# Chunk-selected attention and a soft mixture of experts: combining weights by one exponential, slot maxima in two bf16 parts, slot outputs by column halves

## The chip, the cores and the metric

The kernel is one program on one core of a Trainium2 chip. The metric is the device time of one execution in microseconds (us), as the median of several runs; a measurement of this kernel can tell a difference of about 0.2% from no change. All durations of single instructions come from one profiled execution, which has a time of its own. The engines are PE (matrix multiplication; PEld is its weight loading), DVE (VectorE), ACT (ScalarE), POOL (GpSimd) and SP (SyncE, which here only issues transfers).

## The reference: what is computed

Attention over 4 batches of 8 heads, 768 positions of width 64; each query sees only the keys of its 6 best chunks of 32 (by an upper bound of the score), and causally. The result `x` (3072 rows of 512) goes through a soft mixture of 8 experts with 4 slots each:

```python
logits = x @ phi                                  # 3072 x 32 slots
d = np.exp(logits - logits.max(0))                # dispatch: softmax over rows, for each slot
d /= d.sum(0) + 1e-09
slot_input = (d.T @ x).reshape(E, S_per_e, D)     # 8 experts x 4 slots x 512
for e in range(E):
    h = np.maximum(slot_input[e] @ w1[e], 0.0)    # 512 -> 1024
    slot_out[e] = h @ w2[e]                       # 1024 -> 512
c = np.exp(logits - logits.max(1))                # combine: softmax over slots, for each row
c /= c.sum(1) + 1e-09
return c @ slot_out                               # 3072 x 512, fp32
```

## The kernel before

**The body.** Sixteen pairs of heads, four for each batch, run through one software pipeline. For each pair: transposes of k and q, chunk bounds, selection (MAX8 on DVE), scores on PE, exponentials on ACT, causal masks on POOL, the product with v on PE, normalisation on DVE. The order of the steps is written out by hand as strings (L712 to L717): `PLAIN`, `LOGITS`, `SLOTS`, `AFTER` in turn, `BEFORE_LAST` and `FINAL` for the last two pairs. Each engine works its own instructions in just that order, so an instruction that waits holds all behind it on its engine.

**The mixture's steps in the body.** When a batch's four pairs are through, its mixture steps are sown into the strings. `moe_logits` forms the logits, `moe_copy` (L451, L452) their maximum for each partition, `pm_pad`, and a copy. In the next pair `moe_max` (L458) transposes `pm_pad` on PE in fp32, `moe_bound` (L465) reduces it to `mb`, one value for each slot, and `moe_exp` (L471) spreads `mb` over all partitions by an fp32 matmul with the identity and takes the running maximum (L476, L478). `moe_comb` (L506, L508) subtracts each row's maximum, `moe_comb2` calls `exp_c`, which writes the combining weights; `moe_dispatch` (L531, L535) forms the slot inputs. This is done for batches 0, 1 and 2 at about 53, 81 and 110 us. The last batch goes through its own code behind the last pair (L804 to L839), where `mneg` (L811) is the negated maximum, spread by fp32 matmuls into the logits themselves (L820) and into `bc` (L825).

**The combining weights' layout.** The 32 slots of a row don't stand next to each other in what is multiplied later. `c_pad` has four groups of 32 columns for each row tile. In group j, columns 0 to 3 hold expert j, 4 to 11 experts 4 + j and 5 + j, 12 to 15 expert 4. The same slot thus stands in several places: a slot's output may be summed up from parts that four column groups of PE form side by side, and where no part is formed the factor is zero. `live` marks the lanes of which each slot's sum of weights is taken once.

**The tail.** `experts_in` (L873) multiplies the slot inputs by w1, `relu` (L880) and `hidden_T` (L885, L889) give the transposed hidden values in `hT_pad`. Three functions then form the slot outputs, 512 columns in two halves `y` of 256: `experts_out` (L912) for experts 0 to 3, both halves in one matmul of 512 columns into `so_ps`; `shared_out` (L937) for experts 5 to 7, whose work is shared out over the four column groups; `last_expert_out` (L947) for expert 4. Half 1 goes on into `so_ps`, half 0 into `so_last`. `hidden_T` has two parts `f`, and so have the first two functions. `slot_sums` (L893) gives `zinv`, the inverse of the dispatch sums, from `zrow`, which DVE (L854) and POOL (L859, L860) fill in the layout above. When half 1 is complete, ACT scales it (L992) and stores what `experts_out` left of half 0 (L993, `so_part`); `out_half` then multiplies it by the combining weights of six double tiles of rows (L981), scales them on DVE and ACT (L970, L967) and writes each from SP (L983). Then follows half 0 for the same rows, closed by DVE's fused multiply-add (L1000), and then the other rows with all 512 columns (L1010, L1014, L1016).

The order of that stretch, which the change rewrites:

```python
    experts_out(0)
    hidden_T(1)
    shared_out(1, 0)
    slot_sums()
    experts_out(1)
    shared_out(1, 1)
    last_expert_out(1)
```

Of the kernel before, what the change touches and what calls it, by code (L numbers as in the profile page):

```python
# [59 lines left out]
def kernel(  # L60
# [21 lines left out]
    LAST = NPAIR - 1  # L82

# [36 lines left out]
    pm_pad = static.tile([P, P], F32, name="pm_pad")  # L120
    ns_t = [static.tile([P, NJ, 2, 2, CH], BF16, name=f"ns_t{i}") for i in range(2)]
# [325 lines left out]

    def moe_copy(b):
        lg = small.tile([P, NQT, NS], F32, name="lg", tag="lg")
        ps = st.pop(("lgps", b))  # L450
        nc.vector.tensor_reduce(pm_pad[:, :NS], ps.rearrange("p t s -> p s t"), axis=AX.X, op=ALU.max)  # L451
        nc.vector.tensor_copy(lg, ps)  # L452
        st["lg", b] = lg

    def moe_max(b):

        pmT = p_tp.tile([P, P], F32, name="pmT_ps", tag="tp")
        nc.tensor.matmul(pmT, lhsT=pm_pad, rhs=identf, is_transpose=True)  # L458
        st["pmT", b] = pmT

    def moe_bound(b):
# [4 lines left out]
        st["mb", b] = mb  # L466

    def moe_exp(b):
        lg = st.pop(("lg", b))
        bc = p_tp.tile([P, NS], F32, name="bc_ps", tag="tp")  # L470
        nc.tensor.matmul(  # L471
            bc, lhsT=st.pop(("mb", b)).broadcast_to([P, P]), rhs=identf[:, :NS], start=True, stop=True,
        )
# [40 lines left out]
    def exp_c(lc):  # L514
        c4 = lc[:, :NQT].rearrange("p t (j s) -> p t j s", s=SPE)
        nc.scalar.activation(c_pad[:, :, :, :SPE], c4[:, :, :4], func=ACT.Exp)
# [112 lines left out]
    load_w(1)  # L629

# [18 lines left out]
    nc.vector.memset(pm_pad, 0.0)  # L649
    qneg(2)  # L650
    qpos(2)

    def step(i, what):
# [47 lines left out]
        else:  # L701
# [3 lines left out]
                "moe_max": moe_max, "moe_bound": moe_bound, "moe_comb": moe_comb, "moe_exp": moe_exp,  # L705
# [7 lines left out]
    LOGITS = """sc:0 trk sc:2 ex:0 ex:2 ub norm sc:3 evk lv mk:0 ex:3 pv:0 pv:5 mk:2 pv:1 sc:1 sel xt trq pv:2:3 ex:1 evq sc:5 ex:5 mk:1 kmin sc:4 evx ns moe_logits@2 lw kmax bd evns mk:3 qsn ex:4 mk:5 mk:4 pv:4 lkq moe_copy@2 qsp"""  # L713
    SLOTS = """sc:0 ex:0 moe_max@3 mk:0 sc:1 ex:1 mk:1 ub moe_bound@3 norm sel trk moe_comb@3 evk sc:2 pv:0 pv:1:2 lkq ex:2 sc:3 moe_exp@3 ex:3 mk:3 trq xt pv:3 kmin mk:2 evqd moe_exp2@3 evx kmax bd moe_scale@3 lw sc:4 ex:4 lv mk:4 sc:5 moe_comb2@3 ex:5 mk:5 ns pv:5:4 evns moe_dispatch@3 qsn qsp"""
# [4 lines left out]
    for i in range(1, NPAIR):  # L719
        if i >= EARLY:  # L720
# [94 lines left out]
    def cinv(n):  # L815
# [3 lines left out]
    rep = identf[:NS, :NS].rearrange("p (o s) -> p o s", o=1)  # L819
    nc.tensor.matmul(  # L820
        lg2, lhsT=mneg.broadcast_to([NS, P]), rhs=rep.broadcast_to([NS, NQT, NS]),
        start=False, stop=True, skip_group_check=True,
    )
# [28 lines left out]
    for g in range(2):  # L852
        sl = slice(g * 16, (g + 1) * 16)
        nc.vector.tensor_tensor(  # L854
            zrow[:, :, g * SPE:(g + 1) * SPE],
            si_acc[:1, NDG, sl].rearrange("p (j s) -> p j s", j=4),
            z[:1, sl].rearrange("p (j s) -> p j s", j=4), op=ALU.add,
        )
# [23 lines left out]
    def hidden_T(f):  # L882
# [3 lines left out]
        for g in range(2):  # L886
            o = hT_pad[:, f * 4:(f + 1) * 4, g * 4:(g + 1) * 4, g * SPE:(g + 1) * SPE]
# [15 lines left out]
    so_ps = p_at.tile([P, 2, 512], F32, name="so_ps", tag="at")[:, 0, :]  # L903
    so_last = p_sc.tile([P, HD], F32, name="so_last", tag="sc")
    so_part = tail.tile([P, HD], F32, name="so_part")
# [3 lines left out]
    def experts_out(f):  # L909
        for fg in range(f * 4, (f + 1) * 4):  # L910
            for e in range(4):
                nc.tensor.matmul(  # L912
                    so_ps[e * CH:(e + 1) * CH, :], lhsT=hT_pad[:, fg, e, :],
                    rhs=w_sb[E + e][:, fg * Dm:(fg + 1) * Dm], start=(fg == 0), stop=(fg == NFG - 1),
                )

    outs = (so_last, so_ps[:, HD:])
# [7 lines left out]

    def shared_out(y, f):
        for n in range(3):
            for j in range(4):
                e, fg = SHARED[j][n]
                fg += f * 4  # L930
                c0 = e * CH - (SPE if j == e - 5 else 0)
                if e == LATE[-2]:
                    rhs = w_half[e, y][:, fg, :]
                else:
# [5 lines left out]
                    start=(y == 0 and f == 0 and n == 0), stop=False, skip_group_check=(y == 1),  # L940
                )

    def last_expert_out(y):
        c0 = 4 * CH - 2 * SPE
        for fg in range(NFG):
            j = fg % 4
            nc.tensor.matmul(  # L947
                outs[y][j * CH:(j + 1) * CH, :], lhsT=hT[:, fg, c0:c0 + CH],
                rhs=w_half[LATE[-1], y][:, fg, :],
                start=False, stop=(fg >= NFG - 4), skip_group_check=(y == 1),  # L950
# [34 lines left out]
    experts_out(0)  # L985
    hidden_T(1)
    shared_out(1, 0)
    slot_sums()
    experts_out(1)
# [59 lines left out]
```

## Time and profile before

| | |
|---|---|
| median of 3 runs | 158.46 us (158.31 to 158.50) |
| profiled execution, whole | 158.78 us |
| its span | 157.1 us |
| PE, DVE, ACT, POOL busy | 87%, 77%, 77%, 62% of the span |
| combining exponentials of a batch (L516, L519, L520) | 0.27, 0.35, 0.27 us on ACT |
| PE's transpose of the maxima (L458), three times | 0.33 us each |
| PE's spreading of the maxima (L471), three times two passes | 0.29 us for a pass |
| row writes from SP | 14 of 256 KB, 5 of 512 KB |

A row of the timeline gives the start, the duration, the engine, the line, the operation and what it writes and reads; in brackets stands the engine's idle time ahead of it and what ended it. PE's ends are modelled and matmuls overlap, so the starts of successive ones tell more than the durations. A row of the chain of waits gives start, duration, engine, tile and line. A row of the stretches gives, for each engine, its busy time and its number of instructions, then PE's granted clock, the share of the DMA engines, and GB/s.

### The profile page before, as it was taken

To read this page: it belongs to the slowest core of one execution; us is meant where nothing else is said; L and a number is where in the kernel's file an instruction comes from. 1 tells how busy PE (TensorE), PEld (TensorE's weight loads), DVE (VectorE), ACT (ScalarE), POOL (GpSimd) and SP (SyncE) were. 2 spreads that over 40 slices of the span, in tenths; PEclk is the share of its full clock that TensorE was granted. 3 is DMA by queue.
4 is the path that set the end of the run, shared out by engine and by line. 5 is a ranking of instruction groups with operands and counts; after the bars stand their busy time and mean duration, and the time that the engine had idled before them with its cause. 6 is when DMAs were issued, how large, how long until landed. Compare 5 with 4: busy or idle time off the path is not lost.

```text
span 157.1 us, 6041 instructions
## 1 busy us (share of the span) xinstructions
PE 137.4 (87%) x2485; PEld 91.1 (58%) x2486; DVE 121.6 (77%) x442; ACT 121.2 (77%) x172; POOL 97.8 (62%) x196
## 2 busy tenths in 40 slices
PE   7866799999999999999999999999998999877700
PEld 5543456767666676756657676767666854444200
DVE  4758789889899899999989999989952761178820
ACT  3557899999999988999979789998879531277600
POOL 7899861975878786493868866678598780000000
PEclk9999999999999999999999999999999999999975
DMA  5999999999999999999999999999999999949995
GB/s 152 188 187 211 178 210 213 164 192 215 197 209 196 209 194 211 204 220 172 195 173 211 206 214 177 215 195 214 208 206 212 208 194 197 131 169 384 400 422 230
DMA packets 46171, 33.31 MB, mean 212 GB/s; under 512 B 26304, under 2 KB 41664, under 8 KB 46144
## 3 DMA queue, kind: packets, MB, share of 16 engines
q0 software_dynamic: 41328, 25.86, 113.5%
q1 hardware_dynamic: 4816, 7.08, 12.2%
q8 instruction: 19, 0.31, 0.7%
q14 instruction: 8, 0.07, 0.1%
HBM read 52.49 MB, written 6.29 MB: 374 GB/s over the span
## 4 chain that ended last, share of the span: by engine, by line
PE 58%; DVE 22%; ACT 7%; issue 3%; POOL 3%; DMA 2%; DVEq 0%; POOLq 0%; ACTq 0%
PE at_ps L398 11%; PE sc_ps L346 11%; PE sc_ps L356 8%; PE tr_ps L238 6%; ACT e_sb L370 4%; PE xT_ps L420 3%; PE ub_ps L296 3%; DVE mx L317 3%; DVE x_sb L411 3%; ACT o_sb L967 3%; PE h_ps L873 2%; DVE mm L256 2%; DVE mm L262 2%; DMA w_sb<-in_k_dram 2%; PE ns_ps L328 2%
## 5 line engine op out<-in xcount | busy, mean ns | idle before, releaser
L370 ACT ACTIVATE e_sb<-sc_ps 128x768 bf16<-128x768 f32 (+1 forms) x96 | 83.1, 926 | 6.5 <-PE sc_ps L356 5.1
L380 POOL TENSOR_SCALAR_AFFINE_SELECT e_sb<-e_sb 128x256 bf16<-128x256 bf16 x96 | 37.9, 417 | 22.0 <-ACT e_sb L370 21.8
L346 PE MATMUL sc_ps<-qT,kT 64*128 64x384 bf16 (+3 forms) x258 | 37.5, 308 | 2.3 <-ACT e_sb L370 2.0
L356 PE MATMUL sc_ps<-nsT,smask 64*128 64x384 bf16 (+2 forms) x294 | 37.7, 284 | 0.3
L398 PE MATMUL at_ps<-v_t,e_sb 128*128 128x65 bf16 x642 | 27.1, 194 | 0.4 <-DVE x_sb L411 0.2
L398 PEld LDWEIGHTS <-e_sb 128*128 128x128 bf16 x642 | 22.8, 97 | 6.5 <-POOL e_sb L380 2.9
L317 DVE MAX8 mx<-ub_ps 128x8 f32<-128x8 f32 (+1 forms) x192 | 16.9, 164 | 5.8 <-PE ub_ps L306 4.9
L346 PEld LDWEIGHTS <-kT 64*128 64x128 bf16 x258 | 12.6, 93 | 9.5 <-issue 3.5
L356 PEld LDWEIGHTS <-smask 64*128 64x128 bf16 x294 | 14.7, 95 | 3.8 <-issue 1.3
L169 POOL DMA_DIRECT2D v_t<-in_v_dram x16 | 16.6, 1041 | 0.2
L411 DVE TENSOR_TENSOR x_sb<-at_ps,inv 128x768 bf16<-128x768 f32 (+1 forms) x17 | 15.5, 910 | 0.6
L247 ACT COPY kT<-tr_ps 128x768 bf16<-128x768 bf16 x16 | 12.8, 802 | 3.5 <-PE tr_ps L238 3.5
L256 DVE TENSOR_REDUCE mm<-kT 128x24 bf16<-128x768 bf16 x16 | 15.1, 944 | 0.4 <-ACT kT L247 0.4
L262 DVE TENSOR_REDUCE mm<-kT 128x24 bf16<-128x768 bf16 x16 | 15.1, 943 | 0.0
L247 ACT COPY qT<-tr_ps 128x768 bf16<-128x768 bf16 x14 | 11.5, 823 | 3.3 <-PE tr_ps L238 3.3
L145 POOL DMA_DIRECT2D w_sb<-in_moe_w_dram x14 | 10.2, 729 | 0.0
L296 PEld LDWEIGHTS <-qpn 128*128 128x128 bf16 x192 | 6.0, 96 | 6.7 <-issue 3.3
L431 DVE COPY xT_sb<-xT_ps 128x768 bf16<-128x768 bf16 (+1 forms) x15 | 8.0, 536 | 2.2 <-PE xT_ps L420 2.0
L296 PE MATMUL ub_ps<-bd,qpn 128*128 128x48 bf16 x192 | 7.8, 184 | 1.6 <-POOL qpn L276 1.4
L238 PE MATMUL tr_ps<-ident,k_in 128*64 128x128 bf16 x192 | 8.4, 223 | 0.7 <-DVE k_in L585 0.5
L420 PE MATMUL xT_ps<-ident,x_sb 128*128 128x128 bf16 x96 | 8.2, 220 | 0.3 <-DVE x_sb L411 0.3
L238 PE MATMUL tr_ps<-ident,q_in 128*64 128x128 bf16 x192 | 8.4, 223 | 0.0
(155 smaller groups left out, 216.3 us busy)
## 6 DMA issues: line engine op xcount, KB each, us to landing
w_sb<-in_moe_w_dram POOLq DMA_DIRECT2D x14, 1024.0 KB, 12.7
out_dram<-o_sb SPq DMA_DIRECT2D x14, 256.0 KB, 2.5
v_t<-in_v_dram POOLq DMA_DIRECT2D x16, 192.0 KB, 10.6
k_in<-in_k_dram POOLq DMA_DIRECT2D x7, 384.0 KB, 9.3
q_in<-in_q_dram POOLq DMA_DIRECT2D x7, 384.0 KB, 10.4
out_dram<-o_sb SPq DMA_DIRECT2D x5, 512.0 KB, 4.0
w_half<-in_moe_w_dram POOLq DMA_DIRECT2D x8, 256.0 KB, 11.5
w_sb<-in_k_dram SPq DMA_DIRECT2D x1, 384.0 KB, 3.3
```

The source lines that it names most:

```text
L238: nc.tensor.matmul(ps[h * 64:(h + 1) * 64, g, :], lhsT=src[:, h, g * D:(g + 1) * D], rhs=ident, is_transpose=True,)
L247: copy(t.rearrange("d (p g) -> d p g", g=NQT), st.pop((nm + "ps", i)).rearrange("d g p -> d p g"),)
L256: nc.vector.tensor_reduce(mm[:, 0, 0, :], kT, axis=AX.X, op=ALU.min)
L262: nc.vector.tensor_reduce(mm[:, 1, 0, :], kT, axis=AX.X, op=ALU.max)
L296: nc.tensor.matmul(o, lhsT=qpn[:, x, t * P:(t + 1) * P], rhs=bd[:, x], start=(t == 0 and x == 0), stop=False,)
L317: nc.vector.max(mx[:, a, :], ub[:, a, :max(8, 4 * t + 4)])
L346: nc.tensor.matmul(ps[:, h, c:c + w], lhsT=kT[r, kg * P:(kg + 1) * P], rhs=qT[r, qs], start=True, stop=False,)
L356: nc.tensor.matmul(ps[:, h, c + (f - t0) * P:c + (l - t0) * P], lhsT=smask[r, x, kg].rearrange("p a b -> p (a b)"), rhs=nsT[r, (f - x * NJ ...
L370: nc.scalar.activation(e[:, :, :w], st.pop(("scps", i, g))[:, :, :w], func=ACT.Exp, scale=scale)
L380: nc.gpsimd.affine_select(out=e[:, :, c:c + P], in_=e[:, :, c:c + P], compare_op=ALU.is_ge, fill=0.0, base=0, pattern=[[0, 2], [1, P]], ch ...
L398: nc.tensor.matmul(o, lhsT=st["e", i, g][:, h, c:c + P], rhs=v_t[i % NV][:, h, kg, :D + 1], start=(kg == 0), stop=(kg == t),)
L411: nc.vector.tensor_tensor(st["x", b][:, t0:t1, 2 * j:2 * j + 2, :].rearrange("p t h d -> p h t d"), at[:, :, :, :D], inv.broadcast_to([P, ...
```

## The change

Three edits, with what they need.

*One exponential for the combining weights.* `exp_c` writes 24 neighbouring columns for group j: the logits of experts j to j + 5, by one overlapping read. The place of expert e in group j is therefore always 4 (e - j); `window` gives the matching place in `hT_pad`, in which experts 4 to 7 now stand 16 columns in. `live` marks columns 0 to 3 and 16 to 19 of each group; it is built on POOL from `once` and reduced on DVE ahead of the sixth pair. `zrow` is filled by two DVE additions with overlapping reads, without POOL.

*Maxima in two bf16 parts.* The upper 16 bits of an fp32 value are a bf16 (`high`); the rest, `pm_lo`, `mb_lo` or `mneg_lo`, is one more DVE subtraction. The transposes and the spreading matmuls become two bf16 matmuls that add up.

*Halves apart.* `experts_out` takes the half as an argument and forms 256 columns. Everything of half 1 is formed first; half 0 follows after half 1's six output tiles, all of it. `so_part` goes, and half 0 is closed by a plain scaling.

```diff
+    WIN, HOME = 6 * SPE, 4 * SPE
...
-    nc.vector.memset(live, 0.0)
     nc.vector.memset(lc_sb[:, NQT], 0.0)
-    for j in range(4):
-        nc.vector.memset(live[j * CH:j * CH + 2 * SPE, :], 1.0)
...
+    def high(t):
+        return t.bitcast(BF16).rearrange("p (s x) -> p s x", x=2)[:, :, 1]
...
+    def moe_lo(b, eng=nc.vector):
+        eng.tensor_tensor(pm_lo[:, :NS], pm_pad[:, :NS], high(pm_pad)[:, :NS], op=ALU.subtract)
...
-        nc.tensor.matmul(pmT, lhsT=pm_pad, rhs=identf, is_transpose=True)
+        nc.tensor.matmul(pmT, lhsT=high(pm_pad), rhs=ident, start=True, stop=False)
+        nc.tensor.matmul(pmT, lhsT=pm_lo, rhs=ident, start=False, stop=True)
...
-        st["mb", b] = mb
+        mb_lo = small.tile([P, 1], BF16, name="mb_lo", tag="mb_lo")
+        nc.vector.tensor_tensor(mb_lo, mb, high(mb), op=ALU.subtract)
+        st["mb", b] = high(mb), mb_lo
...
-        nc.tensor.matmul(
-            bc, lhsT=st.pop(("mb", b)).broadcast_to([P, P]), rhs=identf[:, :NS], start=True, stop=True,
-        )
+        for n, part in enumerate(st.pop(("mb", b))):
+            nc.tensor.matmul(
+                bc, lhsT=part.broadcast_to([P, P]), rhs=ident[:, :NS], start=(n == 0), stop=(n == 1))
...
-        c4 = lc[:, :NQT].rearrange("p t (j s) -> p t j s", s=SPE)
-        nc.scalar.activation(c_pad[:, :, :, :SPE], c4[:, :, :4], func=ACT.Exp)
-        pairs = c4[:, :, 4:8]
-        pairs = bass.AP(pairs.tensor, pairs.offset, [list(x) for x in pairs.ap[:-1]] + [[1, 2 * SPE]])
-        nc.scalar.activation(c_pad[:, :, :, SPE:3 * SPE], pairs, func=ACT.Exp)
-        nc.scalar.activation(
-            c_pad[:, :, :, 3 * SPE:4 * SPE], c4[:, :, 4:5].broadcast_to([P, NQT, 4, SPE]), func=ACT.Exp)
+        c4 = lc[:, :NQT].rearrange("p t (j s) -> p t j s", s=SPE)[:, :, :4]
+        runs = bass.AP(c4.tensor, c4.offset, [list(x) for x in c4.ap[:-1]] + [[1, WIN]])
+        nc.scalar.activation(c_pad[:, :, :, :WIN], runs, func=ACT.Exp)
...
+    once = static.tile([P, 8], BF16, name="once")
+    nc.gpsimd.memset(once, 1.0)
+    for sign, base in ((1, 0), (-1, SPE - 1)):
+        nc.gpsimd.affine_select(
+            out=once, in_=once, compare_op=ALU.is_ge, fill=0.0, base=base,
+            pattern=[[-sign * HOME, 8]], channel_multiplier=sign,
+        )
...
     nc.vector.memset(pm_pad, 0.0)
+    nc.vector.memset(pm_lo, 0.0)
...
-    LOGITS = """... lkq moe_copy@2 qsp"""
-    SLOTS = """sc:0 ex:0 moe_max@3 mk:0 sc:1 ..."""
+    LOGITS = """... lkq moe_copy@2 moe_lo@2 qsp"""
+    SLOTS = """sc:0 ex:0 mk:0 moe_max@3 sc:1 ..."""
...
+        if i == NPB + 1:
+            nc.vector.tensor_reduce(live, once, axis=AX.X, op=ALU.max)
...
-    nc.tensor.matmul(
-        lg2, lhsT=mneg.broadcast_to([NS, P]), rhs=rep.broadcast_to([NS, NQT, NS]),
-        start=False, stop=True, skip_group_check=True,
-    )
+    mneg_lo = small.tile([NS, 1], BF16, name="mneg_lo", tag="mneg_lo")
+    nc.vector.tensor_tensor(mneg_lo, mneg, high(mneg), op=ALU.subtract)
     bc = p_tp.tile([P, NS], F32, name="bc_ps", tag="tp")
-    nc.tensor.matmul(
-        bc, lhsT=mneg.broadcast_to([NS, P]), rhs=identf[:NS, :NS], start=True, stop=True,
-    )
+    for n, part in enumerate((high(mneg), mneg_lo)):
+        nc.tensor.matmul(
+            lg2, lhsT=part.broadcast_to([NS, P]), rhs=rep.broadcast_to([NS, NQT, NS]),
+            start=False, stop=(n == 1), skip_group_check=True,
+        )
+        nc.tensor.matmul(
+            bc, lhsT=part.broadcast_to([NS, P]), rhs=ident[:NS, :NS], start=(n == 0), stop=(n == 1),
+        )
...
-    nc.gpsimd.tensor_copy(zrow[:, :3, 2 * SPE:3 * SPE], zrow[:, 1:, SPE:2 * SPE])
-    nc.gpsimd.tensor_copy(
-        zrow[:, :, 3 * SPE:4 * SPE], zrow[:, :1, SPE:2 * SPE].broadcast_to([1, 4, SPE]))
+    for n, c, w in ((4, 0, WIN - SPE), (3, WIN - SPE, SPE)):
+        nc.vector.tensor_tensor(
+            zrow[:, :n, c:c + w], windows(si_acc[:1, NDG, :], n, c, w), windows(z[:1], n, c, w), op=ALU.add)
...
-    so_ps = p_at.tile([P, 2, 512], F32, name="so_ps", tag="at")[:, 0, :]
+    so_ps = p_at.tile([P, 2, 512], F32, name="so_ps", tag="at")[:, 0, :HD]
...
-    def experts_out(f):
+    outs = (so_last, so_ps)
+
+    def experts_out(y, f):
         for fg in range(f * 4, (f + 1) * 4):
             for e in range(4):
+                w0 = fg * Dm + y * HD
                 nc.tensor.matmul(
-                    so_ps[e * CH:(e + 1) * CH, :], lhsT=hT_pad[:, fg, e, :],
-                    rhs=w_sb[E + e][:, fg * Dm:(fg + 1) * Dm], start=(fg == 0), stop=(fg == NFG - 1),
+                    outs[y][e * CH:(e + 1) * CH, :], lhsT=hT_pad[:, fg, e, :],
+                    rhs=w_sb[E + e][:, w0:w0 + HD], start=(fg == 0), stop=False,
                 )
...
+    def window(e, j):
+        return e * CH + HOME - (e - j) * SPE
...
-    experts_out(0)
+    experts_out(1, 0)
+    shared_out(1, 0)
     hidden_T(1)
-    shared_out(1, 0)
     slot_sums()
-    experts_out(1)
+    experts_out(1, 1)
     shared_out(1, 1)
     last_expert_out(1)
-    nc.scalar.activation(so_sb[1], so_ps[:, HD:], func=ACT.Copy, scale=zinv)
-    nc.scalar.activation(so_part, so_ps[:, :HD], func=ACT.Copy, scale=zinv)
+    nc.scalar.activation(so_sb[1], outs[1], func=ACT.Copy, scale=zinv)
     TAGS = (("tp", "tp"), ("sc", "at"))
     for m in range(BYHALF):
         out_half(m, 1, TAGS[m % 2])
-    shared_out(0, 0)
-    shared_out(0, 1)
+    for f in range(2):
+        experts_out(0, f)
+    for f in range(2):
+        shared_out(0, f)
     last_expert_out(0)
-    nc.vector.scalar_tensor_tensor(so_sb[0], so_last, zinv, so_part, op0=ALU.mult, op1=ALU.add)
+    nc.vector.tensor_scalar_mul(so_sb[0], outs[0], zinv)
```

More of the change, by code (lines that the diff above doesn't have):

```diff
@@ L851, with windows @@
     nc.vector.tensor_reduce(z[:1], st.pop("zt")[:1].rearrange("p t s -> p s t"), axis=AX.X, op=ALU.add)
[L852 to L853 removed]
+    def windows(t, n, c, w):
+        return bass.AP(t.tensor, t.offset + c, [list(t.ap[0]), [SPE, n], [1, w]])
+    for n, c, w in ((4, 0, WIN - SPE), (3, WIN - SPE, SPE)):
         nc.vector.tensor_tensor(
[L855 to L858, printed above, removed]
[L859 to L861 removed]
+            zrow[:, :n, c:c + w], windows(si_acc[:1, NDG, :], n, c, w), windows(z[:1], n, c, w), op=ALU.add)
     cT = cT_all.rearrange("p (m a) (c x) -> p m x (a c)", a=2, x=2)
@@ L930, in shared_out @@
                 fg += f * 4
-                c0 = e * CH - (SPE if j == e - 5 else 0)
+                c0 = window(e, j)
                 if e == LATE[-2]:
@@ L939, in shared_out @@
                     rhs=rhs,
-                    start=(y == 0 and f == 0 and n == 0), stop=False, skip_group_check=(y == 1),
+                    start=False, stop=False,
                 )
     def last_expert_out(y):
-        c0 = 4 * CH - 2 * SPE
         for fg in range(NFG):
             j = fg % 4
+            c0 = window(LATE[-1], j)
             nc.tensor.matmul(
```

15 lines of the change are left out of this document (7 added, 8 removed).

## The prediction

> **What bounds the kernel now.** I read the chain of waits first, then, from the end backwards, the stretches of the output phase, SyncE's queue and the timeline of the tail, and last the three places where the softmax maxima are formed.
>
> ```profile
> span 157.1 us, 6041 instructions
> PE 58%; DVE 22%; ACT 7%; issue 3%; POOL 3%; DMA 2%; DVEq 0%; POOLq 0%; ACTq 0%
> 139.50:139.75 0.25, 0.25 (x3) 0.01 (x1) 0.25 (x1) 0.15 (x2) 0.00 (x0) 1.00 0.37 135
> 139.75:140.00 0.25, 0.25 (x13) 0.24 (x16) 0.25 (x2) 0.25 (x2) 0.00 (x0) 1.00 1.08 385
> 145.00:146.00 1.00, 0.10 (x4) 0.10 (x5) 0.84 (x2) 0.10 (x1) 0.00 (x0) 1.00 1.09 381
> 155.25:155.50 0.25, 0.00 (x0) 0.00 (x0) 0.00 (x0) 0.00 (x0) 0.00 (x0) 0.50 0.62 230
> ```
>
> The last two columns of a stretch are the DMA share and GB/s. Writing starts at about 139.7, shows no pause in any stretch that I read (a share over 1.0, 381 GB/s and more), and ends at about 155.25 + 0.62 x 0.25 = 155.4, in a stretch without any compute. So the end of the span is a transfer end, and it moves only with the moment from which the writes run without a gap.
>
> ```profile
> 138.36 8.05 SPq L983 DMA_DIRECT2D out_dram<-o_sb  x12
> 142.45 0.58 SPq L983 DMA_DIRECT2D out_dram<-o_sb  x1
> DMA to landing us min/median/max: 2.5/2.5/2.7
> 137.82 2.63 ACT L967 ACTIVATE o_sb<-oh_ps,inv_a 128x256 f32<-128x256 f32 x6
> 141.90 2.62 ACT L967 ACTIVATE o_sb<-oh_ps,inv_a 128x256 f32<-128x256 f32 x6 [1.46 <-PE oh_ps L981]
> ```
>
> The twelve half-row writes are issued at a steady (8.05 - 0.58) / 11 = 0.68 us. Six belong to column half 1, six to half 0. One scaling of ACT is 0.47 us long (row of L992 below, same width), so the first write is ready at 138.29 and goes at 138.36: 0.07 later. The seventh is the first of half 0: ready at 141.90 + 0.47 = 142.37, so it can go at 142.44; by the 0.68 rhythm it could go at 138.36 + 6 x 0.68 = 142.44; it goes at 142.45. Both limits meet: an earlier half 1 alone only opens a gap ahead of the seventh write, and a later half 0 delays the end at once. That is the reading on which all else rests.
>
> **The change, part by part.** First the slot outputs. Before, half 1 waits for matmuls of 512 columns that also form half 0.
>
> ```profile
> 133.16 1.04 PE L912 MATMUL so_ps<-w_sb,hT_pad 128*32 128x512 bf16 x16
> 133.39 0.60 ACT L880 ACTIVATE h_sb<-h_ps 128x512 bf16<-128x512 f32 x1 [1.53 <-PE h_ps L873]
> 134.13 0.41 PE L885 MATMUL hT_ps<-ident,h_sb 128*128 128x128 bf16 x4
> 134.59 0.29 DVE L889 COPY hT_pad<-hT_ps 128x64 bf16<-128x64 bf16 x2 [1.90 <-PE hT_ps L885]
> 135.23 1.05 PE L912 MATMUL so_ps<-w_sb,hT_pad 128*32 128x512 bf16 x16
> 136.10 0.28 PE L937 MATMUL so_ps<-w_sb,hT_pad 128*32 128x256 bf16 x3
> 136.43 0.39 PE L947 MATMUL so_ps<-w_half,hT_pad 128*32 128x256 bf16 x8
> 136.88 0.47 ACT L992 ACTIVATE so_all<-so_ps,zinv 128x256 bf16<-128x256 f32 x1 [2.89 <-PE so_ps L947]
> 139.75 0.56 PEld L937 LDWEIGHTS <-hT_pad 128*32 128x32 bf16 x24 [0.25 <-issue]
> 140.93 0.48 DVE L1000 SCALAR_TENSOR_TENSOR so_all<-so_last,zinv,so_part 128x256 bf16<-128x256 f32 x1 [0.55 <-ACT o_sb L967]
> ```
>
> Prices: sixteen 512-column matmuls hold PE 136.10 - 135.23 = 0.87; twelve of 256 columns 136.43 - 136.10 = 0.33, so four (they run side by side) take 0.11 and sixteen take 0.44. New order for half 1: experts from 133.16 to 133.60, shared to 133.93; the transposes must await the ReLU, which ends at 133.99, so they start at 134.08 (134.13 before) and end at 134.49. The first of the two copies of L889 (0.29 for both, some 0.17 for one) is done at 134.70, the matmuls go on at 134.77 (135.23 before); the slot-sum matmul, 0.31 long, lies under that copy. Then 0.44 + 0.33 + 0.39 = 1.16 gives 135.93, and ACT's scaling starts at 135.98 against 136.88: half 1 is 0.90 earlier. Removing so_part (ACT) and GpSimd's two copies gains nothing: ACT's first output scaling waits for PE, the copies end 4 us ahead of use.
>
> Half 0: PE took it up at 139.75, 2.40 after half 1 was ready (136.88 + 0.47 = 137.35), held by the output buffers that ACT and DVE free; that stays. Behind it now stand 64 matmuls instead of 32: 8 x 0.11 = 0.88 more. So half 0 is -0.90 + 0.88 = -0.02, and its closing operation, a scaling in place of a fused multiply-add (0.48), gains some 0.03. Sum for the seventh write: -0.05. Bounds: -0.25 (a switch between matmul shapes less) to +0.45 (weight loads set the pace of the narrow matmuls: 24 loads take 0.56, 0.023 each, no more than 0.11 for four, so I stay with the row).
>
> Second, the last batch's maximum. DVE's split adds a short operation, the wide fp32 matmul becomes two bf16 passes:
>
> ```profile
> 126.62 0.28 DVE L811 TENSOR_REDUCE mneg<-pmT_ps 32x1 f32<-32x129 f32 x1
> 127.64 0.33 ACT L829 ACTIVATE d_sb<-lgt_ps 128x192 bf16<-128x192 f32 x1 [2.60 <-PE lgt_ps L820]
> 128.03 0.76 PE L531 MATMUL si_ps<-d_sb,x_sb 128*128 128x32 bf16 x24
> ```
>
> The split starts at 126.93 and takes some 0.17 (a little under L549's 0.19 below), the second pass starts at 127.17 and takes about 0.27 (a 256-column one has 0.28 above), so ACT starts at some 127.51: -0.13, and PE's dispatch at 128.03 and everything behind it with it. Bounds -0.25 and +0.10.
>
> Third, the other three batches, where DVE gains two operations (pm_lo, mb_lo) and PE drops fp32 work:
>
> ```profile
> 20.74 0.17 DVE pm_pad L649
> 52.87 0.33 PE L458 MATMUL pmT_ps<-identf,pm_pad 128*128 128x128 f32 x1
> 53.23 0.29 DVE L465 TENSOR_REDUCE mb<-pmT_ps 128x1 f32<-128x128 f32 x1 [0.22 <-PE pmT_ps L458]
> 53.44 0.22 DVE L410 RECIPROCAL inv<-at_ps 128x12 f32<-128x12 f32 x1
> 56.03 0.34 DVE L506 TENSOR_REDUCE rm<-lg 128x6 f32<-128x192 f32 x1
> 56.35 0.19 DVE L476 COPY m_run<-bc_ps 128x32 f32<-128x32 f32 x1
> 62.73 0.71 PE at_ps L398 x18
> 84.53 0.41 PE L471 MATMUL bc_ps<-identf,mb 128*128 128x32 f32 x2
> 84.98 0.19 DVE L478 TENSOR_TENSOR m_run<-m_run,bc_ps 128x32 f32<-128x32 f32 x1 [0.26 <-PE bc_ps L471]
> 110.90 0.28 DVE L465 TENSOR_REDUCE mb<-pmT_ps 128x1 f32<-128x128 f32 x1
> 111.13 1.06 DVE L317 MAX8 mx<-ub_ps 128x8 f32<-128x8 f32 x12
> 115.03 0.75 PE L531 MATMUL si_ps<-d_sb,x_sb 128*128 128x32 bf16 x24
> 116.56 0.19 DVE L549 TENSOR_TENSOR si_acc<-si_acc,z 128x32 f32<-128x32 f32 x1
> 116.67 0.23 DVE L410 RECIPROCAL inv<-at_ps 128x12 f32<-128x12 f32 x1
> ```
>
> pm_lo has the shape of L549, whose successor starts 0.11 later: 0.11. mb_lo needs the reduction just ahead of it to end; the successor of that started 0.21 (53.23 to 53.44) or 0.23 after the reduction's start, and would now start some 0.35 to 0.40 after it: +0.14 to +0.17. Bounds for the pair 0.11 and 0.45. Batch 0: pm_lo lies in DVE's 0.22 of waiting, two bf16 passes (four take 0.41 at 134.13, so two some 0.28) replace 0.33 and bring the maximum 0.05 earlier, which takes mb_lo's cost down to +0.10 to +0.12, and some 0.04 comes back where the running maximum (0.32 after L506's start at 56.03, where 0.27 would do) waited for PE; DVE then works without rest until PE waits for it at 62.73: +0.08. Batch 1: DVE waits 0.26 for PE's broadcast; two bf16 passes of 32 columns (24 take 0.75 at 115.03) end near 84.8 instead of 84.94, and DVE, which was ready at 84.98 - 0.26 = 84.72 and comes 0.12 later, is ready at 84.84: -0.14. Batch 2: nothing waits for PE, so +0.11 + 0.17 = +0.28 goes from MAX8 (111.13) through the row maximum, GpSimd's subtraction and the exponential to PE's dispatch at 115.03, and I leave 0.01 for what PE had waited: +0.27. The memset of pm_lo follows that of pm_pad, which the chain of waits carries with 0.17 for four times the bytes: +0.07, between 0 and 0.17. The mask that counts slots is built on GpSimd and reduced on DVE while PE is the bound: 0; uncovered it would cost some 0.5 once. The merged exponential:
>
> ```profile
> 59.02 0.28 ACT L516 ACTIVATE c_pad<-lc_sb 128x96 bf16<-128x96 f32 x1
> 59.62 0.80 ACT L370 ACTIVATE e_sb<-sc_ps 128x768 bf16<-128x768 f32 x1
> ```
>
> Three held ACT for 59.62 - 59.02 = 0.60; one over 576 elements should take 0.5 to 0.7 by the widths 96 and 768: 0. Sum of the body: 0.07 + 0.08 - 0.14 + 0.27 = +0.28, bounds -0.2 and +1.0.
>
> [...]
>
> Total: +0.28 - 0.13 - 0.05 = +0.10 on the span. The profiled execution took 158.78 us (span 157.1 and 1.7 around it), 0.32 above the median of 158.46; so 158.88 there and **158.56** in the median: no change that a measurement of this kernel can tell, which is some 0.2% (0.32 us).
>
> **The rivals.** (a) The first write sets the end: if the queue absorbs the gap ahead of the seventh write, the end follows half 1: -0.90 + 0.28 - 0.13 = -0.75, 157.7 us. For it: the writes run without rest from the first on. Against: issue to landing is 2.5 us for each, so no store of issued writes builds up. (b) The body is cheaper than thought, batch 2's chain having slack that the chain of waits does not show: without the 0.27, and with the bounds of the tail, 158.56 - 0.27 - 0.20 = 158.1. (c) Slower: VectorE's two operations cost their full lengths in every batch, 0.19 + 0.21 = 0.40, because each following operation waits for them; it decides where DVE has no idle time to give. Batches 0 and 2 then cost 0.40 - 0.05 - 0.04 = 0.31 and 0.40, batch 1 0.40 - 0.26 = 0.14, the memset 0.17: +1.02 - 0.13 - 0.05 = +0.84, 159.3; from a third of that on it is measurably slower. For it: DVE is on 22% of the chain. Against: L549's row. [...] (d) The halves don't halve: narrow matmuls paced by weight loads, half 1 gains 0.4 less and half 0 pays it: +0.50 for the seventh write, +0.65, 159.1. Against: twelve took 0.33.
>
> **How the numbers follow.** Forecast 0.40; (a) 0.15; (b) 0.10; (c) 0.27; (d) 0.08. So faster 0.25, within 0.2% 0.40, slower 0.35. The range reaches from (a), 157.7, to just short of (c)'s full price, 159.2; the forecast's own is 158.2 to 158.85.
>
> **What would show it.** The first write of half 1 some 0.7 earlier than 138.36, near 137.6; a pause of SyncE of about 0.8 ahead of the seventh write, and that one at 142.5 to 142.6; DMA share dropping for a moment near 143. PE's dispatch in batch 2 at 115.2 to 115.4; the running maximum of batch 1 not later than 85.0. It is wrong if the seventh write goes ahead of 142.1 or behind 142.9, or if the end moves while the seventh write does not.

## The result, and the profile after

The changed kernel takes 159.81 us (median of 19 runs, 159.04 to 161.08), the kernel before 158.83 us in the same comparison (19 runs). The ratio is 1.0065, 95% interval 1.0043 to 1.0087: slower by about 1.0 us. (The intervals of this document reach 0.2 to 0.4% to each side, so differences below that can't be told.) Forecast was no change, 158.56 us in a range of 157.7 to 159.2.

The profiled execution after took 161.07 us, 1.26 above the median, with a span of 159.4. First the first line of its page and SyncE's row writes on the timeline, the seventh on its own:

```profile
span 159.4 us, 6106 instructions
137.79 8.74 SPq L999 DMA_DIRECT2D out_dram<-o_sb  x12
142.63 0.53 SPq L999 DMA_DIRECT2D out_dram<-o_sb  x1
146.63 5.00 SPq L1033 DMA_DIRECT2D out_dram<-o_sb  x5
151.73 2.60 SPq L1031 DMA_DIRECT2D out_dram<-o_sb  x2
```

The first write goes 0.57 earlier than before (138.36), the seventh 0.18 later (142.45), and the end of the span is 2.3 later. So the end moved while the seventh write hardly did. The stretches of the output phase (last two columns: share of the DMA engines, GB/s) tell where, first two of before, then those after:

```profile
141.00:142.00 1.00, 0.53 (x4) 0.41 (x5) 0.62 (x2) 0.10 (x1) 0.00 (x0) 1.00 1.10 386
152.00:153.00 1.00, 0.00 (x0) 0.00 (x0) 0.00 (x0) 0.00 (x0) 0.00 (x0) 0.50 1.04 426
```

```profile
141.00:142.00 1.00, 0.41 (x8) 0.28 (x4) 0.48 (x1) 0.00 (x0) 0.00 (x0) 1.00 1.02 348
143.00:144.00 1.00, 0.79 (x7) 0.51 (x6) 0.93 (x3) 0.90 (x3) 0.00 (x0) 1.00 0.80 271
145.00:146.00 1.00, 0.15 (x3) 0.00 (x0) 1.00 (x2) 0.34 (x1) 0.00 (x0) 1.00 1.02 348
156.00:157.00 1.00, 0.00 (x0) 0.00 (x0) 0.00 (x0) 0.00 (x0) 0.00 (x0) 0.50 0.28 109
157.00:158.00 1.00, 0.00 (x0) 0.00 (x0) 0.00 (x0) 0.00 (x0) 0.00 (x0) 0.50 0.05 20
```

Half rows (pieces of 1 KB) are written at 348 GB/s, where they went at 381 to 386 before, and that already from 141 to 142, ahead of the expected dip at 143. In this one execution the stretches from 156 on also carry only 109 and then 20 GB/s: a few late transfers.

The body lost time too. Rows of TensorE and VectorE around batch 1's maximum, after:

```profile
80.37 0.38 PE L355 MATMUL sc_ps<-nsT,smask 64*128 64x128 bf16 x4
80.57 0.35 DVE L285 TENSOR_SCALAR qpn<-qT 128x768 bf16<-128x768 bf16 x1
81.31 0.23 PE L463 MATMUL pmT_ps<-ident,pm_pad 128*128 128x128 bf16 x1 [0.56 <-DVE qpn L285]
81.63 0.29 DVE L471 TENSOR_REDUCE mb<-pmT_ps 128x1 f32<-128x128 f32 x1 [0.71 <-PE pmT_ps L464]
81.96 0.40 DVE L473 TENSOR_TENSOR mb_lo<-mb 128x1 bf16<-128x1 f32 x1
85.00 0.53 PE L237 MATMUL tr_ps<-ident,q_in 128*64 128x128 bf16 x12 [0.36 <-DVE ns_t L319]
```

and before, the rows of TensorE at the same place:

```profile
81.06 0.33 PE L458 MATMUL pmT_ps<-identf,pm_pad 128*128 128x128 f32 x1
81.76 0.23 PE L346 MATMUL sc_ps<-qT,kT 64*128 64x128 bf16 x2 [0.37 <-issue]
```

TensorE stops in both, for 0.56 and 0.37 us. The bracket after names VectorE's L285, but that had ended at 80.57 + 0.35 = 80.92, 0.39 before TensorE went on: for that long nothing that the profile shows held it. In the changed kernel the stop comes ahead of the transposing matmuls, so VectorE waits 0.71 for them and later TensorE waits 0.36 for VectorE.

### The profile page after: what moved, and what is told of

The parts are those of the page before. It is cut to its first block, busy times and chain, and to the rows that moved or that the text cites. A ratio compares the mean times of both kernels' runs of the same rounds, so it can differ in the third digit from the quotient of the medians.

```text
span 159.4 us, 6106 instructions
## 1 busy us (share of the span) xinstructions
PE 137.1 (86%) x2520; PEld 91.4 (57%) x2521; DVE 121.7 (76%) x446; ACT 120.9 (76%) x163; POOL 98.3 (62%) x197
## 4 chain that ended last, share of the span: by engine, by line
PE 55%; DVE 25%; ACT 5%; POOL 5%; issue 3%; DVEq 0%; POOLq 0%; ACTq 0%
PE sc_ps L345 11%; PE at_ps L397 10%; PE sc_ps L355 7%; PE tr_ps L237 5%; PE xT_ps L419 4%; DVE mx L316 3%; PE ub_ps L295 3%; ACT e_sb L369 3%; DVE x_sb L410 2%; PE h_ps L886 2%; DVE mm L255 2%; DVE mm L261 2%; PE ns_ps L327 2%; ACT o_sb L983 2%; DVE o_sb L986 2%
```

## The experiments

Two things could carry the loss: the body, or the writes. Theory 1 began as "the body, in batch 1", theory 2 as "the writes run slower once they start earlier". The first four runs split the change into its parts. The first three are the kernel before with one edit each, as in the diff above: the halves; the two bf16 parts; the one exponential with its layout. The fourth is the changed kernel with

```diff
-    warm(8)
+    warm(6)
```

> The kernel before, with nothing changed but the column halves of the slot outputs formed apart. Theory 1 (the extra time of the changed kernel comes from the body, where its profile shows TensorE taking the same matmul up 0.38 early before batch 1 and 0.39 late behind it, so 0.77 lost there): this kernel has none of that body, its first write goes some 0.9 us earlier than in the kernel before, its seventh within 0.2, its end too: ratio 0.998 to 1.002. Theory 2 (the writes themselves run slower once they start earlier: the profile of the changed kernel shows 341 to 348 GB/s in the half-row writes against 381 to 387 before): the half-row writes fall below 350 GB/s here too and the end is 1 us or more later: ratio 1.005 to 1.010.

Measured: 158.70 us, ratio 0.9971 (0.9935 to 1.0007). First write 139.45, seventh 144.30: the gap is there, the half rows go at 386 GB/s. Theory 2 falls: an earlier half 1 does not slow the writes. (In this profiled execution TensorE waited 0.84 and 1.05 us for transfers of k and v, up to 68.65 and 77.97; it is read for distances in the tail alone.)

> The kernel before, with nothing changed but the slot maxima in two bf16 parts (all four batches). Theory 1: batch 1 costs some 0.7, batches 0 and 2 some 0.12 each, the last batch gives 0.17 back: 0.75 to 0.85 later at the first write, ratio 1.004 to 1.006. Theory 2: the body is not what costs, so 0.998 to 1.002 with write rates as in the kernel before.

Measured: 160.34 us, ratio 1.0100 (1.0064 to 1.0136), dearer than theory 1 said. The body is not the reason: in this execution TensorE does not stop near 81, and the first write goes at 138.04, 0.32 earlier than before. Yet the half rows go at 345 GB/s.

> The kernel before, with nothing changed but the combining softmax by one exponential over overlapping columns, with the slot window that goes with it and the mask built by GpSimd. Both theories: nothing moves, ratio 0.999 to 1.001; the one ACT operation in place of three lasts 0.5 to 0.7 us. If the ratio is above 1.003, a cost lies here that neither names.

Measured: 160.22 us, ratio 1.0087 (1.0060 to 1.0114). The exponential itself costs what was forecast, as the rows of ScalarE in the changed kernel show:

```profile
58.85 0.68 ACT L525 ACTIVATE c_pad<-lc_sb 128x576 bf16<-128x576 f32 x1
59.42 0.80 ACT L369 ACTIVATE e_sb<-sc_ps 128x768 bf16<-128x768 f32 x1
```

59.42 - 58.85 = 0.57, against 0.60 for three. But the half rows go at 347 GB/s here too: a cost that neither theory names.

> The changed kernel with 6 instead of 8 rounds of the warming matmuls at its start, which puts 8 TensorE instructions fewer ahead of everything that follows. In both profiles so far TensorE stops once, near 81 us, right after its instruction number 2753: in the kernel before that is just behind the transposing matmul of batch 1's maxima, in the changed kernel just ahead of it. Theory 1a (it is this stop, now ahead of the matmul that VectorE waits for, that makes batch 1 dear): here the stop falls behind that matmul again, VectorE's reduction of the maximum no longer waits some 0.7 for TensorE, batch 1 costs 0.0 to 0.3 instead of 0.77, and the time is 0.5 to 0.7 us below the changed kernel's: ratio to the kernel before 1.000 to 1.003. Theory 1b (VectorE's two additional operations cost their full lengths, whatever TensorE does): batch 1 still costs 0.6 or more, ratio 1.005 to 1.009.

Measured: 159.98 us, ratio 1.0045 (1.0007 to 1.0083). TensorE does not stop near 81 at all in this execution, so 1a and 1b are not told apart by it; the table further below does that. Half rows at 347 GB/s.

No changed instruction explains slow writes: the maxima and the exponential change none in common, and the writes are slow with either. What they share is that each adds small tiles to SBUF ahead of the output tiles `o_sb`: `pm_lo` takes 256 bytes of each partition, `mb_lo`, `mneg_lo` and `once` 32 each as they are allocated, and the halves take `so_part`, 1024 bytes, away. Before, the built program places the first output tile at byte 137,984 of the partition, which is 539 x 256, and the other eleven each 4096 bytes further on. Modulo 256 they are shifted by 256 + 32 + 32 = 64 with the maxima, 32 with the exponential, 96 with the whole change, 0 with the halves. Theory 1 now reads: the place of the output tiles decides how fast they are read out. The next runs move nothing but that place (and `so_part`, which lies between, where a kernel still has it), by padding behind `so_all`, which lies ahead of them:

```diff
-    so_all = tail.tile([P, Dm], BF16, name="so_all")
+    so_all = tail.tile([P, Dm + 16], BF16, name="so_all")[:, :Dm]
```

(32 bytes, on the kernel before; 160 and 416 bytes, so `Dm + 80` and `Dm + 208`, on the changed kernel; 224 bytes on a version with the parts of the change that gain.)

> The kernel before with 32 bytes of padding behind so_all, the tile that lies just ahead of the output tiles, so that each output tile starts 32 bytes past a multiple of 256 bytes instead of on one; no instruction differs. Theory 1 (where the output tiles lie decides how fast they are written: the four kernels so far whose added small tiles shifted them, by 32, 64 or 96 bytes past a multiple of 256, wrote half rows at 340 to 348 GB/s, the two whose tiles start on a multiple of 256 at 380 to 387): 340 to 348 GB/s here too, the writes last some 1.25 us longer, time 160.0 to 160.3, ratio 1.007 to 1.010. Theory 2 (the slower writes come with the changed instructions or with single executions): 380 to 387 GB/s, ratio 0.999 to 1.001.

Measured: 160.41 us, ratio 1.0091 (1.0063 to 1.0119): 32 bytes of padding in a kernel whose instructions are all as before cost 1.4 us. Stretches of its output phase:

```profile
141.00:142.00 1.00, 0.61 (x4) 0.41 (x5) 0.62 (x3) 0.35 (x1) 0.00 (x0) 1.00 1.02 343
145.00:146.00 1.00, 0.36 (x7) 0.27 (x8) 0.60 (x3) 0.00 (x0) 0.00 (x0) 1.00 1.01 348
152.00:153.00 1.00, 0.00 (x0) 0.00 (x0) 0.00 (x0) 0.00 (x0) 0.00 (x0) 0.50 1.03 406
```

343 and 348 GB/s, where the kernel before has 386 and 381; the whole rows, written behind them, go at 406, before 426. So the half rows lose about a tenth and the whole rows about a twentieth. The writes of 256 KB (twelve of half rows, two of whole rows), with the median time from issue to landing in us, before and with 32 bytes of padding:

```profile
out_dram<-o_sb SPq DMA_DIRECT2D x14, 256.0 KB, 2.5
out_dram<-o_sb SPq DMA_DIRECT2D x14, 256.0 KB, 3.1
```

Before, all twelve half rows land 2.5 to 2.7 us after their issue, and 256 KB (262,144 bytes) each 0.68 us is 385 GB/s, the rate itself: with the tiles in place the writes keep up with SyncE. Whether they could go faster is not shown, so the tenth is the least that the place costs a half row.

> The changed kernel with 160 bytes of padding behind so_all, so that the output tiles start on a multiple of 256 bytes again (on an odd multiple, as in the kernel before). Theory 1: half rows at 380 to 387 GB/s; what is left of the cost is that of the two bf16 parts in the body (0.3 to 0.5) less the last batch's gain (0.17) and the halves' (0.05): 158.9 to 159.1, ratio 1.000 to 1.002. Theory 2: nothing changes against the changed kernel, ratio 1.005 to 1.009, 340 to 348 GB/s.

> The changed kernel with 416 bytes of padding behind so_all, so that the output tiles start on a multiple of 512 bytes. Theory 1 with 256 bytes as the unit that counts: as with 160 bytes of padding, within 0.2%. If 512 is the unit, the half rows are faster than 390 GB/s and the time is below that of the other by 0.3 us or more. Theory 2: ratio 1.005 to 1.009, as the changed kernel.

Measured: 158.94 us, ratio 1.0001 (0.9965 to 1.0038), and 158.91 us, ratio 0.9987 (0.9952 to 1.0022). The change with its output tiles back on a multiple of 256 takes the time of the kernel before; 512 gives nothing more. (The profiled execution with 160 bytes took 162.12 us, 3.2 above its median, and is read for the rate alone, 381 GB/s.) Stretches with 416 bytes:

```profile
141.00:142.00 1.00, 0.98 (x36) 0.68 (x28) 0.00 (x0) 0.00 (x0) 0.00 (x0) 1.00 1.09 382
144.00:145.00 1.00, 0.79 (x6) 0.48 (x5) 0.94 (x3) 0.90 (x3) 0.00 (x0) 1.00 0.36 125
152.00:153.00 1.00, 0.00 (x0) 0.00 (x0) 0.00 (x0) 0.00 (x0) 0.00 (x0) 1.00 1.01 414
```

382 GB/s again, and the gap ahead of the seventh write (143.51), which the forecast looked for, stands out at 144: a DMA share of 0.36.

> The kernel before with the halves formed apart and the two bf16 parts for the last batch's maximum alone, and 224 bytes of padding behind so_all, which puts the output tiles on a multiple of 512 bytes; the other three batches and the combining softmax are as before. Theory 1: the parts of the change that gain, without those that cost: 0.17 from the last batch and 0.05 from the halves' seventh write on top of clean writes: 158.3 to 158.7, ratio 0.996 to 1.000. Theory 2: the halves or the changed instructions bring slow writes whatever the tiles' place: ratio above 1.004.

Measured: 158.84 us, ratio 0.9978 (0.9944 to 1.0012): as theory 1 has it, and not told from the kernel before. Half rows at 386 GB/s.

The next two ask for the unit and for the price of the bf16 parts by themselves, the kernel before with `Dm + 64` (128 bytes), and the bf16 parts alone with `Dm + 96` (192 bytes).

> The kernel before with 128 bytes of padding behind so_all, so that the output tiles start 128 bytes past a multiple of 256; no instruction differs. If 256 bytes are the unit that counts, the half rows go at 340 to 348 GB/s and the ratio is 1.007 to 1.010, as with 32 bytes. If 128 bytes (or 64, against which the kernel with the maxima alone speaks: its tiles start 64 past) are the unit, 380 to 387 GB/s and 0.998 to 1.002.

Measured: 159.96 us, ratio 1.0075 (1.0043 to 1.0108), 341 GB/s. Among the three tried, the unit is 256 bytes: 512 gives nothing more (382 GB/s with 416 bytes of padding), 128 is too little (341). At 32, 64, 96 and 128 past it the half rows go alike, at 341 to 348 GB/s.

> The kernel before with the slot maxima in two bf16 parts alone, as in an earlier run, now with 192 bytes of padding behind so_all, which puts the output tiles on a multiple of 256 bytes. Theory (place of the tiles): of the 1.0% that the two parts cost without the padding, only what the profiles show before the writes is left: batches 0, 1 and 2 some 0.12, 0.23 and 0.12, the last batch -0.16, so +0.3 us and a ratio of 1.000 to 1.004, with the end 13.0 us behind the seventh write. Rival (the two parts themselves are dear): 1.006 or more.

Measured: 158.98 us, ratio 1.0013 (0.9980 to 1.0046), 383 GB/s. With the tiles in place, nothing is left that this measurement tells from no change.

The last two go after a version that beats both, by closing the gap ahead of the seventh write. Half 0's matmuls stand between half 1's outputs:

```diff
+    experts_out(0, 0)
+    rest = (None, (experts_out, 0, 1), (shared_out, 0, 0), (shared_out, 0, 1), (last_expert_out, 0), None)
     for m in range(BYHALF):
         out_half(m, 1, TAGS[m % 2])
-    for f in range(2):
-        experts_out(0, f)
-    for f in range(2):
-        shared_out(0, f)
-    last_expert_out(0)
+        if rest[m]:
+            rest[m][0](*rest[m][1:])
     nc.vector.tensor_scalar_mul(so_sb[0], outs[0], zinv)
```

> The version with the halves apart, the last batch's maximum alone in two bf16 parts and aligned output tiles, with one thing changed: half 0's 64 matmuls are no longer issued behind all of half 1's outputs, but the first 16 right behind half 1's own (where TensorE waits 0.55 us for the scaling) and the other 48 in four lots between half 1's outputs, where TensorE waits for output buffers. Theory (in all aligned kernels the end comes 13.0 us behind the seventh write, and that one is held by half 0, 0.75 us behind the rhythm of the queue): the gap ahead of the seventh write closes, it goes 4.05 to 4.15 us behind the first instead of 4.84, ratio 0.991 to 0.996. Rival (the lots delay half 1's outputs, since TensorE has no rest there in truth): the first six writes come slower than one in 0.70 us and nothing is gained, ratio 0.997 to 1.001.

Measured: 158.05 us, ratio 0.9963 (0.9922 to 1.0004). From the first to the seventh write (137.50, 141.98) 4.48 us, halfway between theory and the old 4.84: the first six keep their 0.68, but the closing scaling of half 0 comes late. Rows of VectorE:

```profile
140.13 0.48 DVE L976 TENSOR_SCALAR o_sb<-oh_ps,inv_a 128x256 f32<-128x256 f32 x1 [0.17 <-PE oh_ps L987]
140.53 0.48 DVE L1006 TENSOR_SCALAR so_all<-so_last,zinv 128x256 bf16<-128x256 f32 x1
```

It stands behind the sixth output's scaling (L976), which itself waits for TensorE. So, in the last run, it goes first:

```diff
         if rest[m]:
             rest[m][0](*rest[m][1:])
-    nc.vector.tensor_scalar_mul(so_sb[0], outs[0], zinv)
+        if m == BYHALF - 2:
+            nc.vector.tensor_scalar_mul(so_sb[0], outs[0], zinv)
```

> The interleaved version with one line moved: VectorE's closing scaling of half 0 stands right behind half 0's last matmuls, ahead of the sixth half-1 output instead of behind it. In the interleaved run that scaling started at 140.53 though TensorE was done at 139.88, because VectorE had the sixth output's scaling ahead of it, and the seventh write went 4.48 us behind the first where 4.08 is the queue's rhythm. Theory (the seventh write sets the end, 13.0 us ahead of it): 4.05 to 4.15 from the first to the seventh write, the end 13.0 behind the seventh, 0.3 to 0.4 us below the interleaved version, ratio 0.990 to 0.996. Rival (the sixth write is now late by the 0.48 of the scaling ahead of it, and the queue's rhythm breaks there instead): first to seventh 4.4 or more, ratio as before, 0.995 to 0.999.

Measured: 157.78 us, ratio 0.9929 (0.9890 to 0.9967): faster than the kernel before by 1.1 us (0.5 to 1.7), and so than the changed one. From the interleaved version the times don't tell it (the intervals overlap); the closed gap does. Rows of VectorE, then of SyncE:

```profile
139.68 0.48 DVE L1007 TENSOR_SCALAR so_all<-so_last,zinv 128x256 bf16<-128x256 f32 x1
140.09 0.47 DVE L976 TENSOR_SCALAR o_sb<-oh_ps,inv_a 128x256 f32<-128x256 f32 x1
```

```profile
137.25 8.05 SPq L989 DMA_DIRECT2D out_dram<-o_sb  x12
141.35 0.58 SPq L989 DMA_DIRECT2D out_dram<-o_sb  x1
145.41 4.29 SPq L1023 DMA_DIRECT2D out_dram<-o_sb  x5
```

The twelve half writes take 8.05 again, as in the kernel before, without a gap (4.10 from the first to the seventh), and start 1.11 earlier.

The kernels side by side (160 bytes left out, for its profile); GB/s are those of the stretch from 141 to 142 us, the writes' times SyncE's. The 13.0 us of the expectations count from the seventh write to the last bytes written; the table counts to the span's end, about 1.5 us later:

| kernel | output tiles past a multiple of 256 bytes | GB/s | first write | seventh | span's end behind first | behind seventh | ratio |
|---|---|---|---|---|---|---|---|
| before | 0 | 386 | 138.36 | 142.45 | 18.74 | 14.65 | 1 |
| halves alone | 0 | 386 | 139.45 | 144.30 | 19.25 | 14.40 | 0.9971 |
| changed, 416 bytes | 0 | 382 | 138.66 | 143.51 | 19.24 | 14.39 | 0.9987 |
| gaining parts, 224 bytes | 0 | 386 | 136.96 | 141.80 | 19.24 | 14.40 | 0.9978 |
| maxima alone, 192 bytes | 0 | 383 | 139.13 | 143.22 | 18.67 | 14.58 | 1.0013 |
| interleaved | 0 | 384 | 137.50 | 141.98 | 18.90 | 14.42 | 0.9963 |
| interleaved, scaling first | 0 | 386 | 137.25 | 141.35 | 18.65 | 14.55 | 0.9929 |
| before, 32 bytes | 32 | 343 | 138.11 | 142.19 | 19.89 | 15.81 | 1.0091 |
| before, 128 bytes | 128 | 341 | 138.16 | 142.22 | 19.94 | 15.88 | 1.0075 |
| maxima alone | 64 | 345 | 138.04 | 142.09 | 19.86 | 15.81 | 1.0100 |
| exponential alone | 32 | 347 | 138.51 | 142.58 | 19.89 | 15.82 | 1.0087 |
| changed, 6 warm rounds | 96 | 347 | 138.00 | 142.84 | 20.00 | 15.16 | 1.0045 |
| changed | 96 | 348 | 137.79 | 142.63 | 21.61 | 16.77 | 1.0065 |

Two rules can be read off. With the tiles on a multiple of 256, the end stands 14.4 to 14.65 behind the seventh write: the four kernels with a gap ahead of that write have 14.39 to 14.42, the three without 14.55 to 14.65, so a first write that goes up to 0.75 earlier is worth some 0.2 at the end. Off the multiple, the half rows go at 341 to 348 GB/s while SyncE still issues 256 KB each 0.68 us (385 GB/s), so they queue up (with 32 bytes of padding the median from issue to landing is 3.1 us, before 2.5), and the end stands 19.9 to 20.0 behind the first write. That it does so whatever the seventh does rests on one kernel: with 6 warm rounds the seventh goes 4.84 behind the first, in the other four 4.05 to 4.08 (the changed kernel's own profile, with its late transfers, apart).

## Why the prediction was wrong, point by point

**The step that failed** is the one on which all else rested: the end "moves only with the moment from which the writes run without a gap". It took the rate of the writes for given. The change moved the tiles that they read, by sizes that stand in its diff, and the rate fell from some 385 to some 345 GB/s: 19.9 - 18.7 = 1.2 us from the first write to the end. The two kernels that differ from before by padding alone took 1.4 and 1.2 us more (158.8 x 0.0091 and 158.6 x 0.0075). No term of the sum and no rival had a place for that. The prediction's own sign for being wrong, the end moving while the seventh write does not, is what came. The other signs tested when the writes go, and mostly came true: the seventh went 4.84 behind the first, so 0.75 late, and at 142.63. None of these tested how fast they go.

What the runs show of the place: on a multiple of 256 bytes the half rows go at 381 to 386 GB/s, 32 to 128 bytes past it at 341 to 348. From 32 to 128 bytes the price hardly changes (343 and 341 GB/s in the two kernels with padding alone), and its full size is not told, since the aligned writes may be held by SyncE's pace, 256 KB each 0.68 us. What happens inside a transfer that starts off the multiple was not measured; that the place costs it time, these two kernels show.

**The writes' limits** were read rightly for aligned tiles: in halves alone, changed with 416 bytes and gaining parts a first write 4.85 ahead of the seventh gained 0.15 to 0.25 over 4.09 to 4.10, of 0.75. Rival (a), the first write sets the end, holds where the writes are slow. That is why the changed kernel isn't slower still: of the 1.2 us, its earlier first write gives some 0.6 back.

**Half 1** was forecast 0.90 earlier. From the last batch's exponential (L829, L846) to the scaling of half 1 it is 136.30 - 127.99 = 8.31 against 9.24: -0.93. **Half 0**, to its closing operation: 141.16 - 127.99 = 13.17 against 13.29, -0.12, forecast -0.05. Rival (d), halves that don't halve, falls with it (its +0.50 for the seventh write follows from no row: half 1 later by 0.40 makes -0.05 into +0.35). Rows of the changed kernel's timeline in the tail:

```profile
127.13 0.28 DVE L825 TENSOR_REDUCE mneg<-pmT_ps 32x1 f32<-32x129 f32 x1
127.45 0.15 DVE L835 TENSOR_TENSOR mneg_lo<-mneg 32x1 bf16<-32x1 f32 x1
127.99 0.33 ACT L846 ACTIVATE d_sb<-lgt_ps 128x192 bf16<-128x192 f32 x1 [2.44 <-PE bc_ps L842]
136.30 0.47 ACT L1008 ACTIVATE so_all<-so_ps,zinv 128x256 bf16<-128x256 f32 x1 [1.97 <-PE so_ps L963]
141.16 0.48 DVE L1017 TENSOR_SCALAR so_all<-so_last,zinv 128x256 bf16<-128x256 f32 x1 [1.36 <-PE so_last L963]
```

**The last batch's maximum**, forecast -0.13: from `mneg`'s start to the exponential 127.99 - 127.13 = 0.86 against 127.64 - 126.62 = 1.02, so -0.16.

**The body.** Three batches, each as the distance between two groups of TensorE's transposes of x around it (starts, read from the timeline):

| | batch 0: 48.9 to 56.7 | batch 1: 77.0 to 92.7 | batch 2: 105.7 to 112.9 |
|---|---|---|---|
| before | 7.84 | 15.62 (with a stop of 0.37) | 7.19 |
| exponential alone | 7.85 | 15.37 | 7.20 |
| gaining parts, 224 bytes | 7.85 | 15.37 | 7.19 |
| maxima alone | 7.97 | 15.58 | 7.31 |
| maxima alone, 192 bytes | 7.97 | 15.58 | 7.31 |
| changed, 416 bytes | 7.96 | 15.59 | 7.31 |
| changed | 7.96 | 16.39 (with a stop of 0.56) | 7.32 |

Without stops the two parts cost +0.12, +0.21 and +0.12 us: 0.45, where +0.08, -0.14 and +0.27 were forecast, 0.21. The sum is small and off by 0.24. In all three the wait was sought in the wrong place: not the running maximum or the dispatch is late next, but `ns_t`, for which TensorE's next transposes wait. In the kernel with the maxima alone it waits 0.28, 0.31 and 0.19 us there, in the kernel before at none of the three places. Rows of the changed kernel with 416 bytes, batch 1, without a stop:

```profile
82.69 0.29 DVE L471 TENSOR_REDUCE mb<-pmT_ps 128x1 f32<-128x128 f32 x1
83.02 0.23 DVE L473 TENSOR_TENSOR mb_lo<-mb 128x1 bf16<-128x1 f32 x1
83.16 0.22 DVE L409 RECIPROCAL inv<-at_ps 128x12 f32<-128x12 f32 x1
85.88 0.53 PE L237 MATMUL tr_ps<-ident,q_in 128*64 128x128 bf16 x12 [0.30 <-DVE ns_t L319]
```

`mb_lo` costs VectorE 83.16 - 82.69 - 0.21 = 0.26 here, where 0.14 to 0.17 was forecast. In batches 0 and 2 of the kernel with the maxima alone it is 0.18 and 0.16, so there the price was right and only the wait wrong.

The stop's place is what made batch 1 dear in the changed kernel's own profile: 16.39 - 15.59 = 0.80 more than the same instructions without a stop, so theory 1a names what that execution lost and 1b falls. The exponential cost nothing here, as forecast. The mask on GpSimd and the memset of `pm_lo` lie ahead of the table's first mark, near 16 and 20 us, and what they cost is not told: the kernels reach that mark at 48.57 to 50.25, one execution and another. (The prediction gave `pm_pad` four times the bytes of `pm_lo`; it has twice.) The forecast price of an added VectorE operation, its start to its successor's, held: for `pm_lo` 0.09, as rows of VectorE in the changed kernel with 416 bytes show:

```profile
82.16 0.18 DVE L458 TENSOR_TENSOR pm_lo<-pm_pad 128x32 bf16<-128x32 f32 x1
82.25 0.35 DVE L285 TENSOR_SCALAR qpn<-qT 128x768 bf16<-128x768 bf16 x1
```

So rival (c), full lengths and +1.02 for the body, falls: `pm_lo` and `mb_lo` together cost VectorE 0.35 in batch 1, where (c) has 0.40, but TensorE lost 0.21. That each following operation waits for them in full is not what the rows show either: `pm_lo` lasts 0.18, and its successor starts 0.09 after it started. Rival (b), a cheaper body, falls too: 0.45 is dearer than the forecast.

**The sum, with what was measured.** To the first write: 0.45 - 0.16 - 0.93 = -0.64; the slower writes +1.2; together +0.6 us. Measured are +1.0 (0.7 to 1.4) for the changed kernel and +0.7 (0.1 to 1.3) with six warm rounds. The rest, some 0.4 for the changed kernel, is not settled: the stop in batch 1, when it falls ahead of the matmul (16.39 against 15.59, so 0.8), and late transfers at the end would make it up. Both come together in two of the fourteen profiles, the changed kernel's and that with 160 bytes, and in what share of the other executions they come isn't known. With aligned tiles the seventh write counts: 0.45 - 0.16 - 0.12 = +0.2, close to the +0.10 of the prediction (the body was 0.17 dearer than its 0.28, the tail's two terms 0.10 cheaper, so errors in part cancel), and measured as no change.

## What to carry to other kernels

Where a transfer's end sets the time, ask of a change not only when the transfers start but what it does to their source: here the small tiles that the change added moved all output tiles behind them, by 32, 64 or 96 bytes past a multiple of 256 bytes of the partition, and rows of 1 KB that started there were written out a tenth slower (345 to 348 GB/s against 381 to 386), whole rows a twentieth (406 against 426 in the stretch read with 32 bytes of padding). Allocate the tiles that transfers read on such a multiple, by padding if need be, before judging any other edit. And split a change into its parts early: two parts that had no changed instruction in common and slowed the writes alike gave the cause away.

## What the runs showed of the hardware beside it

TensorE's stop near 81 us comes after the same number of instructions in every profile that has it, and not in all. These rows of the stretches, from the start to a moment within the stop, give the number of matmuls and weight loads by then, for the kernel before:

```profile
0.00:81.70 81.70, 75.27 (x1368) 50.28 (x1368) 70.70 (x275) 70.96 (x91) 60.23 (x121) 1.00 1.37 195
```

and for the changed one:

```profile
0.00:81.20 81.20, 75.01 (x1368) 50.10 (x1368) 69.74 (x273) 70.79 (x89) 60.82 (x124) 1.00 1.37 195
```

and for the kernel before with 32 bytes of padding:

```profile
0.00:81.45 81.45, 75.16 (x1368) 50.20 (x1368) 70.60 (x274) 70.91 (x91) 60.10 (x121) 1.00 1.36 194
```

1368 and 1368 each time, and also in the other three profiles that have the stop (halves alone, 160 bytes, interleaved), though in two of the six, the changed kernel's and that with 160 bytes, other instructions stand ahead of that point; the stops last from 0.2 to 0.56 us. Eight of the fourteen profiles show none there. In these six it thus goes with the count of instructions and not with the work, and the change moved the maximum's transpose from just ahead of it to just behind it. The kernel with 6 warm rounds was to move the stop, but its profile has none. What causes it was not shown. The profile lists transfers of instructions as a queue of their own (q8), with one of 0.02 MB between 79 and 80 us both before and after; whether it bears on the stop was not tried.
